# Group norm on one core: the mean moved from VectorE to ScalarE, a staged copy of the scales, and loads and stores cut at other places

## The chip, the cores and the metric

The kernel runs on 1 core of one Trainium2 chip. The metric is the device time of one execution in microseconds (us). Every run lists the core's span (first to last instruction of the program) and the mean granted TensorE clock; all executions quoted here are of the state "fast". The span is about 2 us shorter than the time (637.0 us of 639.18 us in the profiled run of before). Timed comparisons alternate with runs of the kernel before on the same chip.

## The reference, cut to what matters

```python
# x: 128 x 1024 x 32 x 16 bf16; g, b: 1024 bf16; 32 groups of 32 channels
xr = x.reshape(B, G, C // G, H, W)
mu = xr.mean(axis=(2, 3, 4), keepdims=True)
var = ((xr - mu) ** 2).mean(axis=(2, 3, 4), keepdims=True)
xn = ((xr - mu) / jnp.sqrt(var + 1e-5)).reshape(B, C, H, W)
return xn * g[None, :, None, None] + b[None, :, None, None]
```

That is 134 MB in and 134 MB out, each byte once. The work is cut into 32 tiles of 4 MB: 128 partitions (4 samples x 32 groups), each with one group's 32 channels x 512 positions.

## The kernel before

Five engines work by semaphores on a ring of 6 tile buffers. SyncE (SP) issues all large transfers in program order: it stores three tiles, then loads three, and so on. TensorE multiplies a tile by an identity matrix in 32 pieces of 512 columns and so sums them into one 128x512 block in PSUM. VectorE reduces that block to minus the mean (`nm`). ScalarE squares the tile with `nm` as bias, sums, and gets `rstd`. VectorE turns that into 32 scales and 32 biases and scales the tile in place, one channel of 512 columns per instruction, in four quarters; after each quarter it signals `s_done`.

```python
# NT = 32 tiles, NH = 2, NQ = 4, KC = 32 channels, HW = 512, F = KC * HW, SLOTS = 6 buffers, RUN = 3
def load_parts(j):   return NH if j >= NT - IN_PARTS else 1          # the last two tiles in halves
def store_parts(i):  return NQ if i >= NT - IN_PARTS else 2 if i == 1 else 1   # the last two in quarters
# ... SP: 6 loads; then for each tile store(i); after tiles 1, 4, 7, ... the next three loads
# ScalarE, tile i
e.wait_ge(s_mean, i + 3)
for h in range(2):
    e.activation(out=ja[:], in_=ring[:, bass.ds((i % SLOTS) * F + h * (F // 2), F // 2)],
                 func=ACT.Square, bias=nm[:, par : par + 1], accum_out=sq[:, h : h + 1], ...)
# ... var, then rstd -> s_rstd
# VectorE, tile i: the mean of tile i + 1 comes first
e.wait_ge(s_sum, i + 2)
mean(ps[...(i + 1) % 2...], nm[...(i + 1) % 2...])                    # then_inc(s_mean)
e.wait_ge(s_rstd, i + 1)
# ... reciprocal, scl = g / std, bia = b - mean * scl
with nc.Fori(0, NQ, 1, engines=[e.engine]) as q:
    for k in range(KC // NQ):
        c = q * (KC // NQ) + k
        a = ring[:, bass.ds((i % SLOTS) * F + c * HW, HW)]
        e.tensor_scalar(out=a, in0=a, scalar1=scl[:, bass.ds(c, 1)], scalar2=bia[:, bass.ds(c, 1)],
                        op0=ALU.mult, op1=ALU.add)
    e.drain()
    e.sem_inc(s_done, 1)
# ...
```

## Time and profile before

| | before |
|---|---|
| time, median of the first 3 runs | 639.85 us (638.98 to 640.33) |
| span of the profiled run | 637.0 us |
| bytes moved, mean rate | 268.4 MB, 421 GB/s |
| ScalarE and VectorE busy | 76% and 62% of the span |

The page of the kernel before: the span, the DMA row (busy tenths in 40 equal slices) and the GB/s of the same slices, then three groups of instructions (line, engine, operation, output<-inputs, count | busy us, mean ns of one | idle time before them and what ended it).

```profile
span 637.0 us, 7900 instructions
...
DMA  8999999999999999999999999999999999999976
GB/s 362 430 438 416 427 439 438 407 395 428 428 428 434 430 446 430 428 428 430 432 438 442 426 428 430 432 428 444 436 428 428 430 432 434 426 445 431 397 333 270
...
L187 ACT ACTIVATE ja<-ring,nm 128x8192 fp8e5 x64 | 455.8, 7122 | 126.3 <-DVE jd L215 121.5
L246 DVE TENSOR_SCALAR ring<-ring,scl,bia x1024 | 351.0, 412 | 91.6 <-issue 91.6
...
L215 DVE TENSOR_SCALAR_CACHE_REDUCE jd<-ps 128x512 bf16 (+1 forms) x33 | 22.8, 692 | 110.0 <-PE ps L165 88.2
```

DMA is full (9 tenths) from the second slice to the third from the end. ScalarE waits for the mean and VectorE has gaps, but I took neither to matter where DMA is full; `scalar_slower` below bears this out (20.1 us more work on ScalarE, 636.19 us against 635.99). So I looked at where DMA is not full. The windows view of the kernel before gives, for five stretches, each engine's busy time, the granted clock, DMA's busy share and its rate.

```profile
core 0: us, PE busy (x) PEld busy (x) DVE busy (x) ACT busy (x) POOL busy (x), PEclk, DMA share, GB/s
112.00:128.00 16.00, 2.06 (x10) 0.74 (x8) 11.75 (x37) 14.45 (x7) 0.00 (x0) 0.72 0.92 395
600.00:610.00 10.00, 0.00 (x0) 0.00 (x0) 7.78 (x24) 9.85 (x3) 0.00 (x0) 0.50 0.93 398
610.00:620.00 10.00, 0.00 (x0) 0.00 (x0) 7.28 (x24) 4.58 (x4) 0.00 (x0) 0.50 0.83 343
620.00:630.00 10.00, 0.00 (x0) 0.00 (x0) 7.67 (x23) 0.00 (x0) 0.00 (x0) 0.50 0.72 297
630.00:637.00 7.00, 0.00 (x0) 0.00 (x0) 0.80 (x3) 0.00 (x0) 0.00 (x0) 0.50 0.47 194
```

There is a dip at 112 to 128 us (395 GB/s), and a tail from about 600 us in which the rate falls to 343 and 297 GB/s. The waits and the timeline of the kernel before show what compute does near the end (timeline columns: start, duration, engine, line, operation, and in brackets the idle time before it and what ended that).

```profile
ACT ja L187 <- DVE jd L215: 121.5, 31, 19.8
...
DVE jd L215 <- PE ps L165: 88.2, 9, 11.5
```

```profile
556.54 18.85 PE L165 MATMUL ps<-ring,eye 128*128 x80 [32.54 <-POOLq L154]
...
565.36 0.69 DVE L215 TENSOR_SCALAR_CACHE_REDUCE jd<-ps 128x512 bf16 x1 [9.68 <-PE ps L165]
...
567.74 2.75 DVE L246 TENSOR_SCALAR ring<-ring,scl,bia  x8 [0.54 <-issue]
...
582.82 7.12 ACT L187 ACTIVATE ja<-ring,nm 128x8192 fp8e5 x1 [1.28 <-DVE jd L215]
...
599.41 7.12 ACT L187 ACTIVATE ja<-ring,nm 128x8192 fp8e5 x1 [1.29 <-DVE jd L215]
...
628.06 2.74 DVE L246 TENSOR_SCALAR ring<-ring,scl,bia  x8 [0.78 <-issue]
```

TensorE's pass over tile 29 (the first of the last three loads) could start at 556.54 us. VectorE had to take that mean (565.36) before it was allowed to scale tile 28 (567.74), whose statistics ScalarE had ready at 556.2 us: of VectorE's 9.68 us of idle time, some 9.2 us were lost to the order of its program. From then on ScalarE starts a tile every 16.59 us (582.82 to 599.41), and the last quarter is scaled at 630.8 us.

**One DMA engine is late.** In the trace a transfer's semaphore rises 16 times (1,200 such records for the 75 transfers of before), and the page counts 16 DMA engines. I read each record as one engine's, made when its share has landed; that is my reading, which no record confirms. They are not in a view of the profile; this is read from the trace's completion records, before (us):

```
transfer          15 of the engines      the last one
load of tile 0     12.8 to  13.3           13.3
load of tile 11   200.1 to 200.6          201.1
load of tile 17   316.3 to 316.9          320.0
load of tile 23   432.5 to 433.1          438.1
load of tile 29   548.7 to 549.5          556.2
last store        634.5 to 634.7          635.3
```

From about 200 us until the middle of the tail one engine falls further and further behind the other 15. Each wait for a transfer is, in the kernel's code, a wait for all 16, so it is this engine that reloads and the end wait for. I call it the late engine and call its delay against the median of the 16 its lag. The records do not name the engine.

### The profile page before, as it was taken

The numbers are of one execution on the slowest core, as the hardware profiler recorded it, in microseconds if no ns is written. First come the engines' busy times: TensorE is split into PE (matmuls) and PEld (weight loads), VectorE is DVE, ScalarE is ACT, GpSimd is POOL, SyncE is SP. The second block draws the span as 40 slices with busy tenths as digits, with TensorE's granted clock in tenths as the row PEclk, the third lists the DMA queues.
The fourth block names the chain that finished last, engine by engine and source line by source line (L and its number), as shares of the span: only waits on it lengthen the run. The fifth ranks groups of instructions, "written<-read, shape, count | busy, mean of one in ns | idle before, by whom it ended". The sixth has DMA issues, their size and how long they took to land.

```text
span 637.0 us, 7900 instructions
## 1 busy us (share of the span) xinstructions
PE 261.4 (41%) x1025; PEld 108.8 (17%) x1025; DVE 395.4 (62%) x1189; ACT 482.1 (76%) x194; POOL 0.8 (0%) x6
## 2 busy tenths in 40 slices
PE   1886537109503740680087018504810770093000
PEld 0332212003201310230032003201300330041000
DVE  0047777777775677277737764774677277737775
ACT  0598999999997799299939974995799399949950
POOL 0000000000000000000000000000000000000000
PEclk9987668759855985697588559855965795598555
DMA  8999999999999999999999999999999999999976
GB/s 362 430 438 416 427 439 438 407 395 428 428 428 434 430 446 430 428 428 430 432 438 442 426 428 430 432 428 444 436 428 428 430 432 434 426 445 431 397 333 270
DMA packets 10609, 268.45 MB, mean 421 GB/s; under 512 B 1264, under 2 KB 1264, under 8 KB 1264
## 3 DMA queue, kind: packets, MB, share of 16 engines
q1 hardware_dynamic: 10512, 268.44, 98.4%
q10 hardware_dynamic: 96, 0.00, 0.0%
q14 instruction: 1, 0.01, 0.0%
HBM read 134.22 MB, written 134.22 MB: 421 GB/s over the span
## 4 chain that ended last, share of the span: by engine, by line
DMA 56%; DVE 16%; issue 9%; DVEq 8%; PE 7%; ACT 2%; SPq 0%; ACTq 0%; POOLq 0%
DMA out_dram<-ring 35%; DMA ring<-in_x_dram 20%; DVE ring L246 15%; PE ps L165 7%; DVEq L246 3%; DVEq L242 3%; ACT ja L187 2%; DVEq L230 1%; DVE bia L237 1%; DVE scl L233 0%; DVEq L215 0%; DVE inv L231 0%; DVE jd L215 0%; DVEq L250 0%; DVEq L231 0%
## 5 line engine op out<-in xcount | busy, mean ns | idle before, releaser
L187 ACT ACTIVATE ja<-ring,nm 128x8192 fp8e5 x64 | 455.8, 7122 | 126.3 <-DVE jd L215 121.5
L246 DVE TENSOR_SCALAR ring<-ring,scl,bia x1024 | 351.0, 412 | 91.6 <-issue 91.6
L165 PE MATMUL ps<-ring,eye 128*128 x1024 | 261.2, 420 | 307.1 <-POOLq L154 289.7
L165 PEld LDWEIGHTS ps<-ring,eye 128*128 128x128 bf16 x1024 | 108.7, 106 | 459.2 <-issue 366.7
L215 DVE TENSOR_SCALAR_CACHE_REDUCE jd<-ps 128x512 bf16 (+1 forms) x33 | 22.8, 692 | 110.0 <-PE ps L165 88.2
L231 DVE RECIPROCAL inv<-rstd 128x1 f32 x32 | 5.2, 163 | 14.8 <-issue 7.6
L187 ACT ACTIVATION_READ_ACCUMULATOR ja<-ring,nm 128x1 f32 x64 | 11.9, 187 | 0.0
L201 ACT ACTIVATE rstd<-sq,var 128x1 f32<-128x1 f32 x32 | 9.4, 294 | 2.2
L197 ACT ACTIVATE var<-sq,eps_t 128x1 f32<-128x1 f32 x32 | 9.4, 294 | 2.2
L237 DVE SCALAR_TENSOR_TENSOR bia<-scl,nm,gb 128x32 f32<-128x32 f32 x32 | 8.0, 251 | 4.7
L233 DVE TENSOR_SCALAR scl<-gb,inv 128x32 f32<-128x32 f32 x32 | 7.7, 241 | 3.1
L212 DVE COPY gb<-gb_p 128x64 f32<-128x64 f32 x1 | 0.2, 223 | 10.0 <-PE gb_p L159 10.0
L159 PE MATMUL gb_p<-gb_b,rep 32*128 32x64 bf16 x1 | 0.2, 204 | 11.1 <-DMA gb_b<-in_b_dram 11.1
L215 DVE DVE_READ_ACCUMULATOR jd<-ps (+1 forms) x33 | 2.7, 83 | 0.0
L181 ACT ACT_TABLE_LOAD x1 | 1.3, 1283 | 1.9 <-issue 1.9
L159 PEld LDWEIGHTS gb_p<-gb_b,rep 32*128 32x128 bf16 x1 | 0.1, 99 | 11.0 <-issue 11.0
L207 DVE MEMSET ones_b<- 128x128 bf16 x1 | 0.2, 165 | 1.1 <-SPq L253 1.1
L144 POOL TENSOR_SCALAR_AFFINE_SELECT rep<-ones_b 32x128 bf16<-32x128 bf16 x1 | 0.3, 302 | 0.0
L140 POOL TENSOR_SCALAR_AFFINE_SELECT eye<-ones_b 128x128 bf16<-128x128 bf16 x1 | 0.3, 292 | 0.9 <-DVEq L209 0.9
L181 ACT ACTIVATE warm<-eps_t 128x1 f32<-128x1 f32 x1 | 0.2, 203 | 0.0
L273 POOL MEMSET const-bfloat16-1.0<- 128x1 bf16 x1 | 0.1, 101 | 0.0
L273 POOL MEMSET const-uint8-127<- 128x1 uint8 x1 | 0.1, 101 | 0.0
(3 smaller groups left out, 0.3 us busy)
## 6 DMA issues: line engine op xcount, KB each, us to landing
ring<-in_x_dram SPq DMA_DIRECT2D x30, 4096.0 KB, 29.4
out_dram<-ring SPq DMA_DIRECT2D x29, 4096.0 KB, 35.1
ring<-in_x_dram SPq DMA_DIRECT2D x4, 2048.0 KB, 26.7
out_dram<-ring SPq DMA_DIRECT2D x8, 1024.0 KB, 7.5
out_dram<-ring SPq DMA_DIRECT2D x2, 2048.0 KB, 13.0
gb_b<-in_g_dram ACTq DMA_DIRECT2D x1, 2.0 KB, 6.3
gb_b<-in_b_dram ACTq DMA_DIRECT2D x1, 2.0 KB, 9.5
```

The lines of the kernel that those rows point to most:

```text
L165: last = e.matmul(out=ps[:, bass.ds((i % 2) * MM_FREE, MM_FREE)], lhsT=eye[:], rhs=ring[:, bass.ds((i % SLOTS) * F + k * MM_FREE, MM_FREE) ...
L181: e.activation(out=warm[:], in_=eps_t[:], func=ACT.Sqrt)
L187: e.activation(out=ja[:], in_=ring[:, bass.ds((i % SLOTS) * F + h * (F // 2), F // 2)], func=ACT.Square, bias=nm[:, par : par + 1], scale=1.0,
L197: e.activation(out=var[:], in_=sq[:, 0:1], func=ACT.Identity, bias=eps_t[:], scale=inv_n)
L201: e.activation(out=rstd[:, par : par + 1], in_=sq[:, 1:2], func=ACT.Sqrt, bias=var[:], scale=inv_n,).then_inc(s_rstd, 1)
L215: e.tensor_scalar(out=jd[:], in0=ps_i, scalar1=-inv_n, scalar2=None, op0=ALU.mult, op1=ALU.add, accum_out=nm_i,).then_inc(s_mean, 1)
L230: e.drain()
L231: e.reciprocal(out=inv[:], in_=rstd[:, bass.ds(i % 2, 1)])
L233: e.tensor_scalar(out=scl[:], in0=gb[:, 0:KC], scalar1=inv[:], scalar2=None, op0=ALU.mult)
L237: e.scalar_tensor_tensor(out=bia[:], in0=scl[:], scalar=nm[:, bass.ds(i % 2, 1)], in1=gb[:, KC : 2 * KC], op0=ALU.mult, op1=ALU.add,)
L242: with nc.Fori(0, NQ, 1, engines=[e.engine]) as q:
L246: e.tensor_scalar(out=a, in0=a, scalar1=scl[:, bass.ds(c, 1)], scalar2=bia[:, bass.ds(c, 1)], op0=ALU.mult, op1=ALU.add,)
```

## The change

Its intent: take the mean off VectorE, so that VectorE no longer waits for the next tile's sum; ScalarE reads PSUM itself. VectorE copies the 8 scales and 8 biases of a quarter to a fixed place (`cur`), so that each scaling instruction has fewer register addresses. Tile 0 and tile 29 are loaded in halves, tiles 4 and 31 stored in halves, all others whole.

```diff
 def load_parts(j):
-    return NH if j >= NT - IN_PARTS else 1
+    return NH if j in (0, NT - RUN) else 1
 def store_parts(i):
-    return NQ if i >= NT - IN_PARTS else 2 if i == 1 else 1
+    return 2 if i in (4, NT - 1) else 1
 # ScalarE, tile i
-                e.wait_ge(s_mean, i + 3)
+                e.wait_ge(s_sum, i + 1)
+                e.wait_ge(s_done, i * NQ + 1)        # s_done starts at 8
+                e.activation(
+                    out=jm[:], in_=ps[:, par * MM_FREE : (par + 1) * MM_FREE],
+                    func=ACT.Identity, scale=-inv_n, accum_out=nm[:, par : par + 1],
+                ).then_inc(s_mean, 1)
+                e.drain()
 # VectorE, tile i
-            e.wait_ge(s_sum, i + 2)
-            mean(ps[:, bass.ds(((i + 1) % 2) * MM_FREE, MM_FREE)], nm[:, bass.ds((i + 1) % 2, 1)])
             e.wait_ge(s_rstd, i + 1)
 # ... scl and bia become sb[:, 0, :] and sb[:, 1, :]
             with nc.Fori(0, NQ, 1, engines=[e.engine]) as q:
-                for k in range(KC // NQ):
+                e.tensor_copy(out=cur[:], in_=sb[:, :, bass.ds(q * KQ, KQ)])
+                e.drain()
+                for k in range(KQ):
 # ...
-                        out=a, in0=a, scalar1=scl[:, bass.ds(c, 1)], scalar2=bia[:, bass.ds(c, 1)],
+                        out=a, in0=a, scalar1=cur[:, 0, k : k + 1], scalar2=cur[:, 1, k : k + 1],
```

(Cut: the semaphores for the halves, the start value of `s_done`, removed buffers.)

More of the change, by code (lines that the diff above doesn't have):

```diff
@@ L19 @@
 FIRST_RUN = 2
-IN_PARTS = 2
 NH = 2
@@ L52 @@
     NMM = F // MM_FREE
+    KQ = KC // NQ
+    DONE0 = 2 * NQ
     assert NT > SLOTS and F % MM_FREE == 0
@@ L65 @@
     ja = sbuf("ja", [P, F // 2], FP8)
-    jd = sbuf("jd", [P, MM_FREE], BF16)
+    jm = sbuf("jm", [P, MM_FREE], BF16)
     ones_b = sbuf("ones_b", [P, P], BF16)
@@ L78 @@
     inv = sbuf("inv", [P, 1], F32)
-    scl = sbuf("scl", [P, KC], F32)
-    bia = sbuf("bia", [P, KC], F32)
+    sb = sbuf("sb", [P, 2, KC], F32)
+    cur = sbuf("cur", [P, 2, KQ], F32)
     ps = nc.alloc_psum_tensor("ps", [P, 2 * MM_FREE], F32)
@@ L87 @@
     ld = [sem(f"ld{s}") for s in range(SLOTS)]
-    ld_more = [sem(f"ldm{s}") for s in range(IN_PARTS * (NH - 1))]
+    ld_more = [sem(f"ldm{s}") for s in range(2)]
     st = [sem(f"st{s}") for s in range(SLOTS)]
@@ L101, in ld_of @@
             return ld[j % SLOTS], 16 * (j // SLOTS + 1)
-        return ld_more[(j - NT + IN_PARTS) * (NH - 1) + c - 1], 16
+        return (ld_more[0] if j == 0 else ld_more[1]), 16
     def store_parts(i):
-        return NQ if i >= NT - IN_PARTS else 2 if i == 1 else 1
+        return 2 if i in (4, NT - 1) else 1
     def slot(i):
@@ L122, in store @@
                 w = F // store_parts(i)
-                e.wait_ge(s_done, NQ * i + NQ // store_parts(i) * (c + 1))
+                e.wait_ge(s_done, DONE0 + NQ * i + NQ // store_parts(i) * (c + 1))
                 e.dma_start(
@@ L172, in on_tensor @@
             last.then_inc(s_sum, 1)
-        e.wait_ge(s_mean, NT + 2)
-        e.sem_inc(s_sum, 1)
     def on_scalar(e):
@@ L184, in on_scalar @@
                 i = i0 + par
-                e.wait_ge(s_mean, i + 3)
+                e.wait_ge(s_sum, i + 1)
+                e.wait_ge(s_done, i * NQ + 1)
+                e.activation(
+                    out=jm[:],
+                    in_=ps[:, par * MM_FREE : (par + 1) * MM_FREE],
+                    func=ACT.Identity,
+                    scale=-inv_n,
+                    accum_out=nm[:, par : par + 1],
+                ).then_inc(s_mean, 1)
+                e.drain()
                 for h in range(2):
@@ L210, in on_vector @@
         e.sem_inc(s_ones, 1)
+        e.sem_inc(s_done, DONE0)
         e.wait_ge(s_gbp, 1)
         e.tensor_copy(out=gb[:], in_=gb_p[:])
-        def mean(ps_i, nm_i):
-            e.tensor_scalar(
-                out=jd[:], in0=ps_i, scalar1=-inv_n, scalar2=None,
-                op0=ALU.mult, op1=ALU.add, accum_out=nm_i,
-            ).then_inc(s_mean, 1)
-        e.wait_ge(s_sum, 1)
-        mean(ps[:, 0:MM_FREE], nm[:, 0:1])
-        e.drain()
-        with nc.Fori(0, NT, 1, engines=[e.engine]) as i:
-            e.wait_ge(s_sum, i + 2)
-            mean(
-                ps[:, bass.ds(((i + 1) % 2) * MM_FREE, MM_FREE)],
-                nm[:, bass.ds((i + 1) % 2, 1)],
-            )
+        with nc.Fori(0, NT, 1, engines=[e.engine]) as i:
             e.wait_ge(s_rstd, i + 1)
@@ L233, in on_vector @@
             e.tensor_scalar(
-                out=scl[:], in0=gb[:, 0:KC], scalar1=inv[:], scalar2=None, op0=ALU.mult
+                out=sb[:, 0, :], in0=gb[:, 0:KC], scalar1=inv[:], scalar2=None, op0=ALU.mult
             )
@@ L237, in on_vector @@
             e.scalar_tensor_tensor(
-                out=bia[:], in0=scl[:], scalar=nm[:, bass.ds(i % 2, 1)],
+                out=sb[:, 1, :], in0=sb[:, 0, :], scalar=nm[:, bass.ds(i % 2, 1)],
                 in1=gb[:, KC : 2 * KC], op0=ALU.mult, op1=ALU.add,
@@ L242, in on_vector @@
             with nc.Fori(0, NQ, 1, engines=[e.engine]) as q:
-                for k in range(KC // NQ):
-                    c = q * (KC // NQ) + k
-                    a = ring[:, bass.ds((i % SLOTS) * F + c * HW, HW)]
+                e.tensor_copy(out=cur[:], in_=sb[:, :, bass.ds(q * KQ, KQ)])
+                e.drain()
+                for k in range(KQ):
+                    a = ring[:, bass.ds((i % SLOTS) * F + (q * KQ + k) * HW, HW)]
                     e.tensor_scalar(
-                        out=a, in0=a, scalar1=scl[:, bass.ds(c, 1)], scalar2=bia[:, bass.ds(c, 1)],
+                        out=a, in0=a, scalar1=cur[:, 0, k : k + 1], scalar2=cur[:, 1, k : k + 1],
                         op0=ALU.mult, op1=ALU.add,
```

## The prediction

> **What bounds it now.** DMA. The slice rows show DMA at 9 tenths until the last two of 40 slices; 268.4 MB in a span of 637.0 us is 421 GB/s. On the timeline a tile takes 16.59 us of VectorE and ScalarE, its load plus store about 19.5 us. The completion records in the trace (16 per transfer[...]) say more: from about 180 us on, 15 engines land together and one lands later, 3.1 us late at 317 us, 6.7 us at 549 us, 7.5 us at 598 us. The 15 need about 9.71 us per 4 MB tile, the late one about 9.87 us. Loads, slot reuse and the end wait for all 16, so the late engine sets the time: 64 x 9.87 = 632 us plus 2 us to first data; its last landing is at 635.3 us. The 15 idle in the tail (windows view: 343 and 297 GB/s from 610 to 630 us) and land last at 634.6 us, VectorE having ended at about 631.2 us. So two limits nearly coincide at the end: the late engine (635.3) and compute (634.6). [...] the 15 engines' pace is 432.
>
> **What the change does.**
> - VectorE loses the mean (0.69 us plus about 0.2 us) and the order "mean of the next tile before scaling this one". Tile 28's scaling waited 9.7 us for TensorE's pass over tile 29; that goes.
> - Scaling ops start 0.33 us apart, 0.18 + 0.05 us of it two register steps; one is left. Estimate: 0.26 us, so 0.6 us less per quarter, against about 0.4 us for the staged copy. VectorE's tile: about 15 us.
> - ScalarE gains the mean. [...] 512 elements cost an estimated 0.7 us, 0.95 us with accumulator read and gap. Its unhindered tile, 15.26 us, becomes 16.2 us: ScalarE sets the compute pace.
> - First tile in halves: first store some 2.5 us earlier. Tile 4's store in halves closes the dip at 112 to 128 us (395 GB/s), worth about 0.5 us on the late engine, 2 us on the others.
> - Tail: tile 29 in halves, no coupling, 16.2 us pace: compute ends near 625 us instead of 631. But the last store is halves, not quarters: 2 MB need about 6.8 us after compute (estimate from 4.1 us for 1 MB): about 632 us.
>
> **On the critical path.** Compute's tail gains 3 us or more, but the late engine keeps its backlog and ends at about 634.5. Only its idle moments (about 1 us) come back.
>
> **Prediction: 638.6 us**, range 635.5 to 641.0; faster by over 2%: 0.02, within 2%: 0.96, slower by over 2%: 0.02.
>
> **What would show it.** The mean on ScalarE near 0.7 us; ScalarE's tile 16.0 to 16.4 us when not waiting for data; scaling ops 0.2 to 0.3 us apart; no VectorE wait on TensorE; VectorE done by 622 to 627 us; DMA full through the dip at 112 us; the last landing belonging to one late engine never idle in the tail.
>
> **What would make it wrong.** If the late engine's lag differs (nothing in the program that I can name causes it), the tail's gain would show, to 633 us. If the coarser stores leave DMA idle in the tail, the gain vanishes.

639.85 us before, less some 1.25 us, is 638.6 us. The 432 is in GB/s: 4.19 MB in 9.71 us. ScalarE's 0.7 us: an estimate from the page of before gives the same; `ACTIVATE` takes 294 ns for one element per partition and 7122 ns for 8192, so 294 + 511 x 0.834 = 720 ns for 512. With the accumulator read (187 ns) and a gap of 0.06 us that is about 0.95 us, and 15.26 + 0.95 us is the 16.2 us. The 0.4 us for the copy was my estimate, which no trace had shown; in the change it came to 0.17 us for the copy and 0.33 us from there to the scaling instruction.

## The result

The changed kernel takes 635.99 us (median of 4 runs, 635.61 to 636.25); the kernel before, in the same rounds, 640.0 us. The ratio is 0.994 with a 95% interval of 0.9922 to 0.9957: 0.6% faster, well clear of noise and far from 2%. Ratios here are the mean time of one kernel's fast runs over that of the other's of the same rounds, so not quite the ratio of the medians.

The page of the changed kernel, the same rows and the groups that answer to those above (line 186 is the mean on ScalarE, line 237 the staged copy):

```profile
span 634.5 us, 7220 instructions
...
DMA  8999999999999999999999999999999999999985
GB/s 364 430 432 428 430 430 430 430 436 426 434 438 436 434 430 430 430 430 432 438 432 436 434 434 430 430 430 430 436 434 434 432 436 421 440 430 430 430 359 226
...
L195 ACT ACTIVATE ja<-ring,nm 128x8192 fp8e5 x64 | 455.8, 7122 | 11.3 <-issue 6.7
...
L241 DVE TENSOR_SCALAR ring<-ring,cur x1024 | 342.0, 407 | 41.7 <-issue 41.7
...
L186 ACT ACTIVATE jm<-ps 128x512 bf16<-128x512 f32 x32 | 18.9, 590 | 86.7 <-PE ps L166 85.5
...
L237 DVE COPY cur<-sb 128x16 f32 x128 | 22.4, 175 | 54.9 <-issue 54.9
```

The mean costs ScalarE 590 ns. The scaling instruction takes 407 ns instead of 412. The copy adds 128 instructions and 22.4 us of busy time. All told the program issues 7,220 instructions instead of 7,900. The windows view of the changed kernel, the same stretches:

```profile
core 0: us, PE busy (x) PEld busy (x) DVE busy (x) ACT busy (x) POOL busy (x), PEclk, DMA share, GB/s
112.00:128.00 16.00, 0.00 (x0) 0.00 (x0) 12.00 (x39) 15.40 (x9) 0.00 (x0) 0.52 0.99 424
600.00:610.00 10.00, 0.00 (x0) 0.00 (x0) 7.35 (x25) 6.95 (x4) 0.00 (x0) 0.50 0.76 328
610.00:620.00 10.00, 0.00 (x0) 0.00 (x0) 7.57 (x26) 0.00 (x0) 0.00 (x0) 0.50 0.94 403
620.00:630.00 10.00, 0.00 (x0) 0.00 (x0) 2.64 (x8) 0.00 (x0) 0.00 (x0) 0.50 0.71 300
630.00:634.50 4.50, 0.00 (x0) 0.00 (x0) 0.00 (x0) 0.00 (x0) 0.00 (x0) 0.50 0.03 13
```

The dip at 112 to 128 us is gone (424 GB/s). After 630 us almost nothing is moved by the 16 engines together (share 0.03), and yet the span goes on until 634.5 us. The waits and the timeline of the changed kernel:

```profile
DVE inv L225 <- ACT rstd L209: 125.0, 32, 26.5
ACT jm L186 <- PE ps L166: 85.5, 9, 15.0
```

```profile
549.66 8.72 PE L166 MATMUL ps<-ring,eye 128*128 x32 [25.89 <-POOLq L155]
...
557.74 0.17 DVE L237 COPY cur<-sb 128x16 f32 x1 [0.49 <-issue]
558.24 2.67 DVE L241 TENSOR_SCALAR ring<-ring,cur  x8 [0.33 <-issue]
...
561.40 0.17 DVE L237 COPY cur<-sb 128x16 f32 x1 [0.49 <-issue]
...
574.81 0.60 ACT L186 ACTIVATE jm<-ps 128x512 bf16<-128x512 f32 x1
...
590.91 0.58 ACT L186 ACTIVATE jm<-ps 128x512 bf16<-128x512 f32 x1
...
619.97 2.67 DVE L241 TENSOR_SCALAR ring<-ring,cur  x8 [0.32 <-issue]
```

VectorE now waits only for `rstd`. ScalarE's tile is 16.10 us (574.81 to 590.91). A quarter on VectorE is 3.66 us (557.74 to 561.40), longer than before (3.51 us). VectorE ends at 622.6 us, some 8 us earlier than before. The completion records of the changed kernel (us):

```
transfer                        15 of the engines      the last one
load of tile 29, second half    546.4 to 547.4 *         554.2
last store (half of tile 31)    628.8 to 629.0           632.8
```

(* 14 of them; a second engine was at 550.1.) The 15 engines land 5.7 us earlier than before, the late one only 2.5 us. So the end is the late engine's, by 3.8 us.

### The profile page after: what moved, and what is told of

It is laid out like the page before. It is cut to its first block, busy times and chain, and to the rows that moved or that the text cites. A ratio compares the mean times of both kernels' runs of the same rounds, so it can differ in the third digit from the quotient of the medians.

```text
span 634.5 us, 7220 instructions
## 1 busy us (share of the span) xinstructions
PE 263.8 (42%) x1025; PEld 109.3 (17%) x1025; DVE 385.7 (61%) x1251; ACT 502.7 (79%) x258; POOL 0.8 (0%) x6
## 4 chain that ended last, share of the span: by engine, by line
DMA 46%; ACT 29%; DVE 7%; PE 6%; DVEq 5%; issue 4%; ACTq 1%; SPq 0%; POOLq 0%
DMA out_dram<-ring 32%; ACT ja L195 27%; DMA ring<-in_x_dram 14%; DVE ring L241 6%; PE ps L166 6%; DVEq L245 2%; DVEq L241 2%; ACT jm L186 1%; DVE cur L237 1%; DVEq L236 1%; ACT var L205 1%; ACTq L204 0%; ACTq L195 0%; ACT rstd L209 0%; DVE sb L231 0%
## 5 line engine op out<-in xcount | busy, mean ns | idle before, releaser
L195 ACT ACTIVATE ja<-ring,nm 128x8192 fp8e5 x64 | 455.8, 7122 | 11.3 <-issue 6.7
L241 DVE TENSOR_SCALAR ring<-ring,cur x1024 | 342.0, 407 | 41.7 <-issue 41.7
L186 ACT ACTIVATE jm<-ps 128x512 bf16<-128x512 f32 x32 | 18.9, 590 | 86.7 <-PE ps L166 85.5
L237 DVE COPY cur<-sb 128x16 f32 x128 | 22.4, 175 | 54.9 <-issue 54.9
L231 DVE SCALAR_TENSOR_TENSOR sb<-sb,nm,gb 128x32 f32<-128x32 f32 x32 | 8.0, 251 | 4.8 <-issue 0.2
L227 DVE TENSOR_SCALAR sb<-gb,inv 128x32 f32<-128x32 f32 x32 | 7.7, 241 | 2.5
L186 ACT ACTIVATION_READ_ACCUMULATOR jm<-ps 128x1 f32 x32 | 6.2, 193 | 0.0
```

The costliest lines, as they stand in the source:

```text
L186: e.activation(out=jm[:], in_=ps[:, par * MM_FREE : (par + 1) * MM_FREE], func=ACT.Identity, scale=-inv_n, accum_out=nm[:, par : par + 1], ...
L227: e.tensor_scalar(out=sb[:, 0, :], in0=gb[:, 0:KC], scalar1=inv[:], scalar2=None, op0=ALU.mult)
L231: e.scalar_tensor_tensor(out=sb[:, 1, :], in0=sb[:, 0, :], scalar=nm[:, bass.ds(i % 2, 1)], in1=gb[:, KC : 2 * KC], op0=ALU.mult, op1=ALU.add,
L237: e.tensor_copy(out=cur[:], in_=sb[:, :, bass.ds(q * KQ, KQ)])
L241: e.tensor_scalar(out=a, in0=a, scalar1=cur[:, 0, k : k + 1], scalar2=cur[:, 1, k : k + 1], op0=ALU.mult, op1=ALU.add,)
```

## The experiments

All runs gave correct results. Two questions: is the end really the late engine's and not compute's, and why did the late engine itself end earlier than I had said? Theory L in the expectations is "the late engine's backlog sets the end"; theory C is "the end of VectorE plus the last store". The lag's growth below is measured between about 190 and 548 us, where DMA is full (9 tenths in every page and DMA view that was printed).

### The two parts apart: `compute_only`, `transfers_only`

```diff
 # compute_only: the changed kernel with
-    load_parts:  NH if j in (0, NT - RUN)      store_parts: 2 if i in (4, NT - 1)
+    load_parts:  NH if j >= NT - 2             store_parts: NQ if i >= NT - 2 else 2 if i == 1
 # transfers_only: the kernel before with the opposite edit
```

> The change's engines with the transfers of before (loads and stores cut as before). Theory L (the one late DMA engine's backlog sets the end): most of the gain comes with the faster early stores, which close the dip at 112 to 128 us, so 636 to 637.5 us, with VectorE done several us before the last landing and the 15 engines landing 2 us or more before the late one. Theory C (compute's tail plus the last store sets the end): VectorE ends near 625 us and the last store is a quarter of 4 us, so 631 to 634 us, faster than the change itself.

Measured: 637.02 us, ratio 0.996 (0.9947 to 0.9974). VectorE ended at 629.3 us, later than either theory had it: with tile 29 loaded whole, TensorE's pass over it starts at 555.1 us instead of 549.7 and its mean comes at 565.2 us instead of 558.5. The 15 engines landed at 633.2 us, the late one at 633.5. L's number was met, but with the two limits together again, so the run does not decide.

> The engines of before with the loads and stores cut as in the change. Theory L: the late engine sets the end unless compute is later; tile 29 in halves brings VectorE's end 3 to 4 us forward (to about 627 us), the last half store takes about 7 us after it, so 15 engines and the late one land together near 634 us: 636.5 to 638.5 us. Theory C: the same end of VectorE plus 7 us, 636 to 638 us; this run alone does not separate them, it sizes what the cuts are worth without the move of the mean.

Measured: 638.05 us, ratio 0.9972 (0.9959 to 0.9986). VectorE ended at 625.7 us, the 15 engines at 632.0, the late one at 634.0. The two parts are worth 0.4% and 0.3%, together about the 0.6% of the whole. In `transfers_only` the lag grew by 6.5 us, in `compute_only` by 5.4 us (before: 6.7, the change: 4.9). So with the engines' side of the change the late engine falls behind less, which no theory of mine had foreseen.

### Which cut closed the dip: `tile4_whole`

```diff
-    return 2 if i in (4, NT - 1) else 1
+    return 2 if i == NT - 1 else 1
```

> The change with tile 4 stored whole. If the cut of store 4 is what closed the dip at 112 to 128 us: the dip returns (under 410 GB/s) and 0.5 to 2 us come back, 636.5 to 638 us. If VectorE's earlier start alone closed it (the store would be issued near 115 us, while the store ahead of it runs until 120 us): no dip, 635.5 to 636.5 us, same as the change.

Measured: 635.52 us, ratio 0.9933 (0.992 to 0.9947). The dip stays closed, as the windows view of this run shows for that stretch:

```profile
112.00:128.00 16.00, 0.00 (x0) 0.00 (x0) 11.97 (x39) 15.40 (x9) 0.00 (x0) 0.56 0.99 426
```

With the changed engines, then, store 4 is early enough whole; its cut is not needed.

### Slack in compute: `scalar_slower`

```diff
+                e.activation(out=jm[:], in_=ring[:, bass.ds((i % SLOTS) * F, MM_FREE)], func=ACT.Identity)
+                e.drain()
                 e.activation(out=var[:], in_=sq[:, 0:1], func=ACT.Identity, bias=eps_t[:], scale=inv_n)
```

> The change with one more ScalarE instruction per tile (a 128x512 Identity whose output nobody reads, about 0.6 us, in front of the variance), so ScalarE's tile becomes about 16.8 us. It is a test of slack in compute: theory L (the late engine sets the end, compute is 3 to 4 us ahead): VectorE ends 2 to 2.5 us later, the 15 engines land near 631 us and the time stays within 0.5 us of the change: 635.5 to 636.6 us. Theory C (compute's end plus the last store sets the end): 638 to 639 us.

Measured: 636.19 us, ratio 0.9937 (0.9924 to 0.9951), against 0.994 for the change. The page and the timeline of this run show the added work and VectorE's last quarter:

```profile
span 634.5 us, 7284 instructions
...
L205 ACT ACTIVATE jm<-ring 128x512 bf16 x32 | 20.1, 629 | 2.2
```

```profile
622.22 2.67 DVE L245 TENSOR_SCALAR ring<-ring,cur  x8 [0.33 <-issue]
```

ScalarE does 20.1 us more, VectorE ends at 624.9 instead of 622.6 us, the 15 engines land at 631.1 instead of 628.9 us, and the late engine lands at 632.8 us, exactly where it was. The time does not move. That decides for L: in the changed kernel compute has slack at the end, the late engine has none.

### Sparing the late engine its last packets: `last_on_15` (failed)

```diff
-                e.dma_start(out=o_v[i][:, half], in_=slot(i)[:, half])          # second half of tile 31
+                for p, q in ((0, 120), (120, 128)):
+                    e.dma_start(out=o_v[i][p:q, half], in_=slot(i)[p:q, half])
```

> The change, with its last half store cut by rows into 120 and 8[...]. Theory L[...] and the end moves from the late engine (632.3 us) to the others (628.5 us plus one more 0.6 us packet): 632.5 to 634 us. Theory L, and the late engine is another: no gain, 635.5 to 637 us. Theory C (VectorE's end plus the last store): no gain or 0.6 us worse, 636 to 637 us.

I had supposed that the cut could spare the late engine; no run showed this, and the first range of theory L rests on it. The 0.6 us is a packet of 16 KB (611 ns, median of the packet records of the change).

Measured: 638.59 us, ratio 0.9982 (0.9969 to 0.9996): 0.4% worse than the change. The final records came spread over 628.9 to 634.9 us, where the change has 15 at 628.9 and the late engine's at 632.8: the cut by rows made that half store itself slower. It says nothing on which engine is late. The failure is one of the method.

### Are instructions the cause of the lag: `no_stage`, `vector_nops`, `pool_nops`

The kernel before issues 4,048 instructions on VectorE, the change 3,246; the lag grew by 6.7 and 4.9 us. Theory F takes that as cause and effect.

```diff
 # no_stage: the change without the copy
-                e.tensor_copy(out=cur[:], in_=sb[:, :, bass.ds(q * KQ, KQ)])
-                e.drain()
-                ... scalar1=cur[:, 0, k : k + 1], scalar2=cur[:, 1, k : k + 1]
+                ... scalar1=sb[:, 0, bass.ds(q * KQ + k, 1)], scalar2=sb[:, 1, bass.ds(q * KQ + k, 1)]
 # vector_nops: the change with, before each scaling instruction on VectorE,
+                    e.engine_nop()
 # pool_nops: the change with, on GpSimd, after each load that it passes on,
+            with nc.Fori(0, 16, 1, engines=[e.engine]):
+                e.engine_nop()
```

> The change without the staged copy: scales and biases are taken at register addresses again, so each scaling op has two register steps as before, and VectorE issues some 700 more instructions (about 3,950 against 3,246). Theory F (the late DMA engine is delayed in proportion to the instructions that VectorE issues; 4,048 of them went with 6.4 to 6.7 us of lag from 190 to 548 us, 3,246 with 4.9 to 5.4 us): the lag grows back to about 6.4 us in that stretch and the last landing comes about 2 us later, 637.5 to 639 us. Rival P (only the pace of the compute engines and the cut of the transfers matter): VectorE's quarter is 0.1 to 0.2 us shorter without the copy, ScalarE sets the pace anyway: 635 to 636.3 us, as the change.

Measured: 637.07 us, ratio 0.9951 (0.9937 to 0.9964), with 640 instructions more than the change. The lag grew by 5.3 us. Slower, but less than F said. P is wrong too: VectorE's quarter takes 3.70 us without the copy, not less than the 3.66 us with it.

> The change with one empty instruction in front of each of the 1,024 scaling ops on VectorE; no data is moved or computed by them. Theory F: 1,024 more instructions, about 4,270: the lag from 190 to 548 us grows to 6.5 to 7 us and the last landing comes 2.5 to 3 us later: 638 to 639.5 us, provided that VectorE itself still ends before 626 us. Rival P: 635.5 to 636.5 us as long as VectorE keeps up with ScalarE (16.1 us a tile); if the empty instructions cost VectorE over 0.1 us each, it becomes the pace and the run says nothing.

Measured: 637.78 us, ratio 0.9963 (0.995 to 0.9977). The page of this run:

```profile
span 635.6 us, 8244 instructions
...
L242 DVE TENSOR_SCALAR ring<-ring,cur x1024 | 351.5, 410 | 45.7 <-issue 45.7
```

The 1,024 empty instructions make each scaling instruction 3 ns longer and set them 0.334 us apart instead of 0.324. VectorE's tile became 16.54 us, so VectorE did become the pace of compute by a little, against the proviso. VectorE ended at 625.5 us, the 15 engines at 631.7 us, the late one at 633.9 us, 1.1 us later than in the change's profile. The lag grew by 5.9 us. `scalar_slower` showed that VectorE may end at 624.9 us without any effect, and here too the 15 engines are done 2.2 us before the late one: the slower compute does not set the end, so the delay goes with the instructions.

> The change with 16 empty instructions in a loop (some 48 instructions with the loop's own) after each load seen by GpSimd, about 1,500 instructions more on an engine that is idle and touches none of the data. If instructions of any engine delay the late DMA engine: its lag from 190 to 548 us grows from 4.9 to 6 us or more and the time to 637 to 638 us. If it is VectorE's instructions alone: 635.6 to 636.4 us and the lag as in the change.

Measured: 637.53 us, ratio 0.9964 (0.995 to 0.9977). The lag grew by 5.4 us, less than I had set as the mark, but the time is 0.24% up on the change, as with the empty instructions on VectorE. GpSimd touches none of the data, and VectorE and ScalarE kept the change's pace (16.10 us a tile; VectorE's end, 623.8 us, is 1.2 us later because the last loads landed later). So it is not VectorE's instructions alone. One instruction fetch (at 165.9 us) came on top in this run; at that time the lag rose by 0.4 us, as in the change.

### Fewer instructions: `unrolled`, `six_tiles`, `six_first`, `six_first_pe`

```diff
 # unrolled: VectorE's loops over tiles and quarters written out in full, constant addresses, no copy
-        with nc.Fori(0, NT, 1, engines=[e.engine]) as i:
+        for i in range(NT):
 # six_tiles: written out over the 6 buffers only; tile 4 stored whole
+        with nc.Fori(0, 30, 6, engines=[e.engine]) as i0:
+            for s in range(6): tile(i0 + s, s)         # slot(s), sb[:, 0, c : c + 1] are constant addresses
+        for s in range(2): tile(30 + s, s)
 # six_first: the two odd tiles in front of the loop
+        for s in range(2): tile(s, s)
+        with nc.Fori(2, 32, 6, engines=[e.engine]) as i0:
+            for j in range(6): tile(i0 + j, (2 + j) % 6)
 # six_first_pe: TensorE's loop written the same way
```

> The change with VectorE's loop written out: every address is constant, no register steps, no staged copy, no branches, about 1,500 instructions instead of 3,246. Theory F: the lag from 190 to 548 us falls to about 2.3 us, the late engine no longer ends last by much, 631 to 633.5 us (the 15 others landed at 628.5 us in the change's profile, and VectorE's tile gets shorter by about 2.5 us of which only the last counts). Rival P: the late engine ends where it did, 635 to 636.3 us.

Measured: 639.1 us, ratio 0.9984 (0.997 to 0.9997). My expectation failed, although VectorE's last tile did get shorter (12.3 us against 15.3 us in the change). The DMA view of this run:

```profile
GB/s 362 433 447 397 433 437 438 417 439 425 431 435 442 427 429 429 436 441 429 429 423 431 439 441 430 427 427 440 437 431 429 425 437 427 443 427 427 376 397 150
...
q14 instruction: 13, 0.10, 0.0%
```

Instructions are now fetched during the run: the trace has 11 such fetches between 56 and 615 us, where that of the change, which differs from this run in VectorE's program alone, has none. The late landings step by about 10.7 us instead of 9.7 just after them (for example 203.0 to 213.7 us, fetch at 207.5; 262.1 to 272.7, fetch at 266.5) and by 9.6 to 9.7 us otherwise; the lag of the latest engine rose by about 1.0 us at each, to 10.9 us. Each fetch is recorded with 8 KB, and VectorE's 1,389 instructions came to one fetch per 126. VectorE itself was held up little (between 200 and 570 us five idle gaps of 0.32 to 0.44 us between its instructions, each about 4 us before a fetch); what shows with DMA full is the step of about 1.0 us on a DMA engine. A second engine's lag grew by 4.4 us, as with few instructions in the next run.

> The change with tile 4 stored whole and VectorE's loop written out over the six buffers only: constant addresses for the scaling ops, no staged copy, five passes over a body of some 260 instructions, about 1,420 instructions issued instead of 3,246. The fully written-out loop was slower because its instructions had to be fetched in blocks during the run (11 instruction fetches in the trace's DMA records, and one DMA engine 1 us later at each); a body of this size should be fetched once. If so: no fetch records during the run, no 1 us steps. Theory F (lag in proportion to VectorE's instructions): lag growth from 190 to 548 us of about 2.2 us and 631 to 633 us. If most of the lag has another cause (the second-latest engine of the written-out run still gained 4.4 us): growth near 4.4 us and 634.3 to 635.3 us. If the fetches come back with each pass: 637 us or more.

Measured: 633.54 us, ratio 0.99 (0.9884 to 0.9915): 1.0% faster than the kernel before and faster than the change (intervals apart). 1,430 instructions on VectorE, 5,403 in all; fetches only at 55, 104 and 609 us. (That a loop's body is fetched once was expected from the change, whose loops pass 32 times without a fetch recorded between 0 and 634 us.) The two latest engines' lags grew by 3.0 and 4.5 us. So the time lies between F and the middle expectation: fewer instructions help, by 0.33% against `tile4_whole`, but much of the lag stays.

> The six-buffer loop with the two odd tiles ahead of the loop instead of behind it, so that no instructions have to be fetched near the end. In the previous form a fetch at 609 us went with a step of 10.3 us instead of 9.7 between two late landings. If that fetch cost the late engine its 0.6 to 1 us: no fetch after the first 120 us, last landing near 629.8 us, 632.3 to 633.2 us. If it fell on an engine that was not the last: 633.3 to 633.8 us, the same as before the move.

Measured: 634.26 us, ratio 0.9913 (0.9899 to 0.9927), runs from 633.34 to 634.79 us: not faster than `six_tiles`. The fetch at 609 us was traded for one at 151 us, which the late engine also feels (143.0 to 153.7 us). Inconclusive at this size.

> The same with TensorE's loop written out over the six buffers too, which takes away some 1,000 register instructions of TensorE and nothing else. If instructions of any engine load the late DMA engine (0.3 to 0.9 us per 1,000 in the runs so far): 0.3 to 0.9 us faster than the form with VectorE's loop alone, unless the longer program costs fetches of its own in the first pass. If only VectorE's do: the same within 0.3 us.

Measured: 632.99 us (632.65 to 633.53), ratio 0.9901 (0.9886 to 0.9917): the best median of all, 0.1% below `six_first`; the two intervals overlap, and it is not separate from `six_tiles`. The page and the windows view of this run:

```profile
span 631.0 us, 4268 instructions
...
GB/s 366 432 431 410 436 434 429 432 436 431 436 434 432 428 434 432 432 426 434 432 432 432 432 432 430 432 434 434 434 430 436 434 430 426 440 432 432 432 425 252
...
L247 DVE TENSOR_SCALAR ring<-ring,sb 128x512 bf16<-128x512 bf16 x1024 | 342.1, 407 | 15.2 <-issue 1.3
```

```profile
600.00:610.00 10.00, 0.00 (x0) 0.00 (x0) 5.42 (x18) 4.19 (x4) 0.00 (x0) 0.50 0.99 429
610.00:620.00 10.00, 0.00 (x0) 0.00 (x0) 6.24 (x19) 0.00 (x0) 0.00 (x0) 0.50 0.99 426
620.00:630.00 10.00, 0.00 (x0) 0.00 (x0) 0.00 (x0) 0.00 (x0) 0.00 (x0) 0.50 0.45 193
```

With 4,268 instructions DMA is full until 620 us, and VectorE is done at 616.5 us. Twelve engines land the last store by 624.7 us, four between 627.7 and 629.6 us.

The five pairs that differ in instructions and in little else (for the last two also in VectorE's or TensorE's loop form), time worked out as the difference of the two ratios times 640 us:

| pair | instructions | time | per 1,000 |
|---|---|---|---|
| `no_stage` against the change | +640 | +0.7 us | 1.1 us |
| `vector_nops` against the change | +1,024 | +1.5 us | 1.4 us |
| `pool_nops` against the change | +1,568 | +1.5 us | 1.0 us |
| `six_tiles` against `tile4_whole` | -1,816 | -2.1 us | 1.2 us |
| `six_first_pe` against `six_first` | -1,135 | -0.8 us | 0.7 us |

Each single difference is near the width of its interval (about 0.8 us either way for one ratio), but all five have the same sign, on three engines. The runs of one set of rounds can also be compared directly: `scalar_slower`, which ends as the change does, took 635.71 to 636.27 us, `no_stage` 636.65 to 637.36 and `vector_nops` 637.17 to 637.94, without overlap. That the number of instructions issued delays the late engine is thereby well supported.

**When they do it.** The completion records say more. Between about 190 and 536 us three loads and three stores take turns. Take the late engine's steps, from one landing to its next, and count the instructions that the trace has in each step. An engine that keeps up takes about 9.71 us for a load and 9.67 us for a store; what the late engine takes beyond that is its extra time, here per turn:

| run | three loads: instructions, extra time | three stores: instructions, extra time | per 1,000 in the stores |
|---|---|---|---|
| before | 379, 0.11 us | 355, 0.93 us | 2.6 us |
| `transfers_only` | 377, 0.09 us | 355, 0.90 us | 2.5 us |
| `no_stage` | 418, 0.04 us | 312, 0.79 us | 2.5 us |
| the change | 384, 0.00 us | 286, 0.74 us | 2.6 us |
| `vector_nops` | 439, 0.06 us | 325, 0.83 us | 2.6 us |
| `pool_nops` | 480, -0.01 us | 335, 0.85 us | 2.5 us |

The late engine loses its time while it stores, in proportion to the instructions of all engines issued meanwhile; those issued while it loads cost it little or nothing. As somewhat under half of all instructions fall in the stores, this agrees with the 1 us or so per 1,000 of the first table. `pool_nops` shows it best: its 49 extra instructions after a load fell into two load steps and one store step of each turn; the load steps stayed at 9.70 to 9.72 us, the store step rose from 10.05 to 10.16 us. In `six_tiles` the second-latest engine follows the same line (205 instructions in the stores, 0.54 us). The latest one there is another: it loses some 0.3 to 0.4 us in the third load of a turn, as the second-latest of the change does, for a reason that I did not find. This line was found after the runs, from one profile of each; no run was made to test it.

How instructions do this is open: no fetches are recorded during the runs of the second table (but for the one in `pool_nops`), and every run here, timed ones too, lists a span and a clock, so I can't tell whether the recording of instructions is itself the load. A run without recording would have been the test; none was made.

## Why the prediction was right or wrong

The time (635.99 us) lies within the range (635.5 to 641.0), near its lower edge, and "within 2%" was right. The size of the gain was not: predicted 1.25 us, measured 4.0 us. That the time still fell within the range is owed to the range's width, not to a gain foreseen.

- **What bounds the kernel.** Right. "The late engine sets the time": `scalar_slower` delays compute by 2.3 us and the time stays.
- **ScalarE.** Right: 0.59 us for the mean (0.7 predicted), tile 16.10 us (16.2 predicted).
- **VectorE's scaling.** The step "one register step is left, 0.26 us" failed. In the changed kernel the instructions start 0.324 us apart although the register steps come every 0.224 us and run ahead of them; in `unrolled`, without any, they start 0.324 us apart too. So in these two kernels the register steps do not set that pace, and with the copy a quarter became 3.66 us, not about 3.3. It cost nothing, because ScalarE sets the compute pace.
- **The coupling.** Right: VectorE's wait on TensorE is gone and VectorE ends at 622.6 us (622 to 627 predicted).
- **The dip.** It closed as said, and was worth as little as said to the late engine: by 191 us the other 15 were 2.5 us ahead of their times before, the late one 0.2 us (2 and 0.5 predicted). But "tile 4's store in halves closes the dip" was the wrong cause for this kernel: `tile4_whole` has no dip.
- **The last store.** 6.3 us after VectorE's end (6.8 predicted); the 15 engines at 628.9 us (632 predicted).
- **The term that was mis-sized.** "Only its idle moments (about 1 us) come back": the late engine's last landing came 2.5 us earlier (635.3 to 632.8), not 1. The prediction took its pace of 9.87 us per tile as a property of the chip that "nothing in the program that I can name causes". The runs show that part of it follows from the program: the lag grew by 6.7 us before and 4.9 us after. Of the 2.5 us, 0.2 were there by 191 us, 1.8 came from there to 556 us, 0.5 in the tail. In the stores the change issues 286 instructions a turn instead of 355, which at the rate of the second table is an estimated 1.1 us over some six turns; the rest of the 1.8 us is two long load steps of the kernel before (9.96 and 10.22 us), of unknown cause. The copy, which I had booked as a plain cost, is worth its place for this reason (`no_stage`: 0.7 us slower without it).
- **With the same cuts of the transfers**, the ratios go 0.9972 (`transfers_only`), 0.9951 (plus the mean on ScalarE: `no_stage`), 0.994 (plus the copy: the change). The transfers are thus worth about 1.8 us, the mean's move 1.3, the copy 0.7 (differences of ratios times 640 us). The mean's move takes away only 35 instructions, and yet the growth fell from 6.5 to 5.3 us. The second table gives a reason for an estimated 0.7 us of this: the instructions come at other times, 312 a turn in the stores instead of 355. No run isolated it.
- **Two smaller parts.** The profile of before that I read was among its faster ones: its span was 637.0 us, while the median span of its later runs was 637.6 us. And the time outside the span fell from about 2.1 to 1.75 us.

## What to carry to other kernels

When DMA is full, do not stop at its mean rate: look at when each of the 16 completion records of a transfer comes, because each wait in this kernel is a wait for the latest (6.95 us behind the median of the 16 for the load of tile 29, before). This kernel's compute had slack, and it still gained from issuing fewer instructions (constant addresses in a loop body over the buffers: `six_tiles`, 1,816 fewer than `tile4_whole`, 2.1 us); writing everything out, with 11 fetches during the run, lost (`unrolled`: 639.1 us). In the traces here it was the instructions issued while stores ran that counted. Whether this holds when nothing is recorded was not tested. And test slack directly, by adding work to the engine in question: it costs one run and decides between two limits that end within a microsecond of each other.
